# Next batch's softmax with powers on GpSimd, and a reordered first batch, in a cross-covariance attention plus SwiGLU kernel

## The chip, the cores and the metric

One core of one Trainium2 chip. The metric is the device time of one execution in microseconds (us), by the slowest core, of which there is only one here. Before the change the kernel took 873.5 us (median of 4 runs, 871.9 to 875.4). Runs in a slower state of the chip are marked by the measurement; verdicts use fast runs alone.

## The reference, cut to what matters

```python
B, N, C = 4, 6016, 256;  d_ff = 1536
qn = q / (norm(q, axis=1) + 1e-6)          # norms over the N tokens, one per channel
kn = k / (norm(k, axis=1) + 1e-6)
s  = kn.transpose(0, 2, 1) @ qn / tau      # per batch 256 x 256
a  = softmax(s)                            # (exp, divided by its row sum + 1e-9)
x  = (v @ a).reshape(B * N, C)
out = (silu(x @ w_gate) * (x @ w_val)) @ w_out
```

The kernel never forms `v @ a`. It multiplies the softmax into the two weight matrices (per batch, `Wg = a @ w_gate` and `Wv = a @ w_val`) and then works on `v` directly. So a batch needs the norms, the product of k and q, the softmax and the weight products *before* its first token can be worked on. For batches 1 to 3 this is done in the background of the batch before; batch 0 has to do it in the open.

## The kernel before

A batch is 12 chunks of 512 tokens (the last has 384), a chunk is 12 steps, so a batch has 144 steps and the kernel 576. The three matmul groups of a step are what TensorE does nearly all the time:

```python
def gv_step(b, ci, f, sv):                    # one step: 128 of the 1536 hidden channels
    g_ps, v_ps = ...                          # PSUM, two buffers each
    for dst, W in ((g_ps, Wg), (v_ps, Wv)):
        for kk in range(CH):                  # CH = 2
            nc.tensor.matmul(dst[:, :mv], W[:, kk, fs], vT[:, kk, :mv], ...)
    nc.scalar.activation(silu[:, :mv], g_ps[:, :mv], ACT.Silu)
    nc.vector.tensor_mul(sv[:, f, :mv], silu[:, :mv], v_ps[:, :mv])
# then prev.emit(prev.cm): four output matmuls (o_new) of the chunk before,
# then background(b + 1, step): whatever the plan puts into this step
```

Tokens come in two hops: GpSimd issues a load of v that casts to bf16 into DRAM (`vb`), and SyncE issues a DMA transpose of that into SBUF (`vT`, three buffers). In the program they stand two chunks ahead of their use.

```python
def load_v(b, ci):
    nc.gpsimd.dma_start(out=vb[...], in_=v[b, ...])
    nc.sync.dma_start_transpose(out=vT[:, :, :mv], in_=vb[:mv, :])
```

The background softmax, all in one step of the plan:

```python
def norm_sum(b):
    nc.tensor.matmul(ss, ones_f, acc, ...)                 # column sums, on all partitions
def softmax(b):
    nc.scalar.activation(nrm, ss, ACT.Sqrt)                # 128 x 512
    nc.vector.tensor_scalar_add(ink, in0=nrm[:, 1, :], scalar1=1e-6)
    nc.vector.reciprocal(ink, ink)                         # 128 x 256
    ... qc: norms of q put down the partitions by tiny matmuls ...
    nc.vector.tensor_mul(s_f[:, jh, :], kq[:, jh, :], ink)
    ... inq = 1 / (qc + 1e-6) ...
    nc.scalar.activation(exT[:, jh, :], s_f[:, jh, :], ACT.Exp, scale=inq[:, jh:jh + 1])
    ... rs = row sums of exT, by matmul; smr = 1 / (rs + 1e-9) ...

LOAD0, SQ0 = 2, 18                     # plan: loads of batch b+1 every 6 steps from step 2,
                                       # a pair of norm tiles every 3 steps from step 18,
S1 = SQ0 + 3 * NP + 2                  # then the softmax, then 12 weight products
```

The first batch: all loads of q and k, then `w_gate`, `w_val`, the first v tile, `w_out`, the second v tile; then norms, softmax, the first four weight products, and the steps begin.

## Time and profile before

The page's lines of busy time by engine (us, the share of the span of 869.4 us, the number of instructions) and of the chain of waits, which is the work that ended last followed back to the start, by engine and by line:

```profile
PE 811.8 (93%) x4933; PEld 484.7 (56%) x4933; DVE 545.1 (63%) x844; ACT 477.9 (55%) x841; POOL 77.8 (9%) x151
...
PE 90%; DMA 7%; ACT 1%; DVE 1%; issue 0%; POOL 0%; POOLq 0%
PE g_ps L238 29%; PE o_new L263 28%; PE v_ps L238 28%; DMA q_sb<-in_q_dram 3%; PE ps L221 3%; DMA vT<-vb 2%; PE kq_new L123 2%; DMA vb<-in_v_dram 2%; DVE ink L181 1%; ACT L178 0%; ACT exT L196 0%; PE ss L172 0%; DVE s_f L188 0%; ACT nrm L17
```

TensorE is busy for 93% and makes up 90% of the chain. A faster other engine is worth nothing here unless it closes a gap of TensorE, so the question is where these gaps are. The list of TensorE's waits (engine, line and tile that waited, what it waited for; us in total, times, longest):

```profile
PE g_ps L238 <- DMA vT<-vb: 16.6, 1, 16.6
...
PE rs L201 <- ACT exT L196: 13.2, 8, 3.2
PE qc L184 <- ACT nrm L178: 5.7, 4, 1.7
```

The 16.6 us is one wait, at the start, for the first transposed v tile. The waits on exT and nrm are the four softmaxes, one per batch. (A line left out, 15.9 us, belongs to the first batch too, which is bound by the loads of q and k there.) The start in the timeline (start us, duration us, instruction; in brackets the idle time before it and what ended that):

```profile
28.14 0.53 POOL L104 DMA_DIRECT2D vb<-in_v_dram  x1 [0.54 <-DMA q_sb<-in_q_dram]
...
39.42 0.91 ACT L196 ACTIVATE exT<-s_f,inq 128x256 bf16<-128x256 f32 x2 [1.98 <-DVE inq L191]
...
43.10 26.19 SPq L108 DMA_TRANSPOSE vT<-vb  x3
...
60.67 1.01 PE L238 MATMUL g_ps<-vT,Wg 128*128 128x512 bf16 x2 [16.61 <-DMA vT<-vb]
```

The load of the first v tile was issued at 28.14 us behind two weight matrices; its transpose began at 43.10 and the first step at 60.67. The first output matmul of chunk 1, which I use as the end of the start, stands at 85.40.

One background softmax, TensorE and its helpers:

```profile
195.42 1.02 PE L172 MATMUL ss<-acc_new,ones_f 128*128 128x512 f32 x2
...
197.53 1.28 ACT L178 ACT_TABLE_LOAD   x1
...
199.47 0.74 PE L184 MATMUL qc<-ones_f,nrm 1*128 1x1 f32 x4 [1.73 <-ACT nrm L178]
199.78 1.75 DVE L181 RECIPROCAL ink<-ink 128x256 f32<-128x256 f32 x1
...
203.19 0.19 PE L201 MATMUL rs<-ones_bf,exT 128*128 128x1 bf16 x1 [2.98 <-ACT exT L196]
...
203.68 1.01 PE L238 MATMUL g_ps<-vT,Wg 128*128 128x512 bf16 x2
...
207.72 0.38 PE L238 MATMUL g_ps<-vT,Wg 128*128 128x512 bf16 x1
```

From 195.42 to 207.72 TensorE gets through three steps, which take 3.9 us elsewhere (1.30 us each). So a softmax costs about 8.4 us: ScalarE's table load for Sqrt at 197.53, the square root, the reciprocal of 1.75 us, the products and the exponentials stand one after the other between the column sums (`ss`) and the row sums (`rs`). (The table load for Exp, in a line left out, runs beside the reciprocal; the one for Silu comes after the row sums.) TensorE waits 1.73 and 2.98 us there, and then runs slower for a while (the matmul pair at 203.68 took 1.01 us, usually 0.59; the granted clock was 0.67 between 200 and 210 us).

### The profile page before, as it was taken

To read this page: it belongs to the slowest core of one execution; us is meant where nothing else is said; L and a number is where in the kernel's file an instruction comes from. 1 tells how busy PE (TensorE), PEld (TensorE's weight loads), DVE (VectorE), ACT (ScalarE), POOL (GpSimd) and SP (SyncE) were. 2 spreads that over 40 slices of the span, in tenths; PEclk is the share of its full clock that TensorE was granted. 3 is DMA by queue.
4 is the path that set the end of the run, shared out by engine and by line. 5 is a ranking of instruction groups with operands and counts; after the bars stand their busy time and mean duration, and the time that the engine had idled before them with its cause. 6 is when DMAs were issued, how large, how long until landed. Compare 5 with 4: busy or idle time off the path is not lost.

```text
span 869.4 us, 13410 instructions
## 1 busy us (share of the span) xinstructions
PE 811.8 (93%) x4933; PEld 484.7 (56%) x4933; DVE 545.1 (63%) x844; ACT 477.9 (55%) x841; POOL 77.8 (9%) x151
## 2 busy tenths in 40 slices
PE   5528999997999999997999999998999999999998
PEld 2203666664566566664556566664556666656666
DVE  3505788875655688885555578886465555555554
ACT  4414666665544566665554566665545544444453
POOL 5333331023310000000000000000000000000000
PEclk9957999998999999998999999999999999999999
DMA  9999999239983121120211212121112112212211
GB/s 89 156 146 131 165 149 191 62 50 140 169 188 63 43 61 50 37 61 13 58 37 49 55 49 54 45 49 37 37 34 62 55 50 49 61 49 37 58 37 55
DMA packets 92785, 64.83 MB, mean 75 GB/s; under 512 B 53552, under 2 KB 91440, under 8 KB 91952
## 3 DMA queue, kind: packets, MB, share of 16 engines
q0 software_dynamic: 17456, 27.01, 23.6%
q1 hardware_dynamic: 75264, 36.97, 17.0%
q8 instruction: 38, 0.62, 0.3%
q14 instruction: 27, 0.22, 0.1%
HBM read 78.64 MB, written 36.96 MB: 133 GB/s over the span
## 4 chain that ended last, share of the span: by engine, by line
PE 90%; DMA 7%; ACT 1%; DVE 1%; issue 0%; POOL 0%; POOLq 0%
PE g_ps L238 29%; PE o_new L263 28%; PE v_ps L238 28%; DMA q_sb<-in_q_dram 3%; PE ps L221 3%; DMA vT<-vb 2%; PE kq_new L123 2%; DMA vb<-in_v_dram 2%; DVE ink L181 1%; ACT L178 0%; ACT exT L196 0%; PE ss L172 0%; DVE s_f L188 0%; ACT nrm L178 0%; ACT silu L241 0%
## 5 line engine op out<-in xcount | busy, mean ns | idle before, releaser
L242 DVE TENSOR_TENSOR sv<-silu,v_ps 128x512 bf16<-128x512 bf16 (+1 forms) x576 | 383.0, 674 | 253.2 <-ACT silu L241 230.9
L241 ACT ACTIVATE silu<-g_ps 128x512 bf16<-128x512 f32 (+1 forms) x576 | 338.5, 588 | 322.1 <-PE g_ps L238 303.3
L238 PE MATMUL g_ps<-vT,Wg 128*128 128x512 bf16 (+1 forms) x1152 | 342.4, 379 | 16.6 <-DMA vT<-vb 16.6
L238 PE MATMUL v_ps<-vT,Wv 128*128 128x512 bf16 (+1 forms) x1152 | 341.3, 378 | 0.0
L263 PE MATMUL o_new<-w_out_sb,sv 128*128 128x256 bf16 x2256 | 340.2, 274 | 0.0
L263 PEld LDWEIGHTS <-sv 128*128 128x128 bf16 x2256 | 221.6, 98 | 142.4 <-issue 2.2
L238 PEld LDWEIGHTS <-Wv 128*128 128x128 bf16 x1152 | 113.6, 99 | 133.6 <-issue 5.2
L238 PEld LDWEIGHTS <-Wg 128*128 128x128 bf16 x1152 | 107.8, 99 | 47.5 <-issue 20.7
L167 DVE TENSOR_TENSOR acc_new<-acc_new,sq 128x512 f32<-128x512 f32 x135 | 93.4, 692 | 24.9 <-ACT sq L141 22.6
L136 ACT ACTIVATE sq<-q_sb 128x512 bf16<-128x512 fp8e5 x96 | 57.9, 615 | 17.8 <-DMA q_sb<-in_q_dram 17.8
L123 PE MATMUL kq_new<-k_sb,q_sb 128*128 128x512 fp8e5 x184 | 46.4, 335 | 0.0
L141 ACT ACTIVATE sq<-k_sb 128x512 bf16<-128x512 fp8e5 x72 | 44.2, 614 | 0.0
L272 ACT COPY o_sb<-o_new 128x512 f32<-128x512 f32 x48 | 28.2, 587 | 14.4 <-PE o_new L263 13.7
L96 POOL DMA_DIRECT2D q_sb<-in_q_dram x48 | 26.2, 547 | 91.2 <-PE g_ps L238 50.1
L274 DVE COPY o_sb<-o_new 128x512 f32<-128x512 f32 (+1 forms) x48 | 31.7, 661 | 3.1 <-PE o_new L263 3.0
L153 PE MATMUL ss_new<-sq,ones_bf 128*128 128x512 bf16 x47 | 16.1, 427 | 15.9 <-DVE sq L138 15.9
L96 POOL DMA_DIRECT2D k_sb<-in_k_dram x48 | 25.7, 536 | 33.3 <-DMA k_sb<-in_k_dram 16.2
L123 PEld LDWEIGHTS <-q_sb 128*128 128x256 fp8e5 x184 | 23.9, 141 | 6.4 <-issue 1.9
L104 POOL DMA_DIRECT2D vb<-in_v_dram x48 | 23.8, 495 | 40.8 <-DMA k_sb<-in_k_dram 22.2
L138 DVE TENSOR_TENSOR sq<-k_sb 128x512 bf16<-128x512 fp8e5 (+1 forms) x24 | 15.3, 677 | 18.3 <-DMA k_sb<-in_k_dram 11.8
L221 PE MATMUL ps<-w_gate_sb,exT 128*128 128x512 bf16 x48 | 16.7, 439 | 1.6 <-ACT Wg L224 1.6
L221 PE MATMUL ps<-w_val_sb,exT 128*128 128x512 bf16 x48 | 16.3, 431 | 1.6 <-ACT Wv L224 1.6
(39 smaller groups left out, 102.3 us busy)
## 6 DMA issues: line engine op xcount, KB each, us to landing
out_dram<-o_sb SPq DMA_DIRECT2D x92, 256.0 KB, 2.3
vb<-in_v_dram POOLq DMA_DIRECT2D x44, 256.0 KB, 10.4
q_sb<-in_q_dram POOLq DMA_DIRECT2D x44, 128.0 KB, 10.7
k_sb<-in_k_dram POOLq DMA_DIRECT2D x44, 128.0 KB, 10.9
w_gate_sb<-in_moe_w_gate_dram POOLq DMA_DIRECT2D x1, 768.0 KB, 13.1
w_val_sb<-in_moe_w_val_dram POOLq DMA_DIRECT2D x1, 768.0 KB, 14.9
w_out_sb<-in_moe_w_out_dram POOLq DMA_DIRECT2D x1, 768.0 KB, 17.6
vT<-vb SPq DMA_TRANSPOSE x48, 3.2
```

The source lines that it names most:

```text
L96: nc.gpsimd.dma_start(out=dst[:, gs:gs + gm, :], in_=src[b].rearrange("(p s) c -> p s c", s=NS)[:, gs:gs + gm, :])
L123: nc.tensor.matmul(kq[:, jh, :], q_sb[:, ps:ps + 2, js], k_sb[:, ps:ps + 2, :], start=(t == 0 and jh == 0), stop=last, perf_mode=DR, skip_ ...
L136: nc.scalar.activation(sq[:, :pm, 0, :], q_sb[:, ps:ps + pm, :], ACT.Square)
L141: nc.scalar.activation(sq[:, :pm, 1, :], k_sb[:, ps:ps + pm, :], ACT.Square)
L167: nc.vector.tensor_add(acc, acc, sq[:, s, :, :])
L221: nc.tensor.matmul(ps, exT[:, jh, ih * P:(ih + 1) * P], src[:, jh, cols], start=(jh == 0), stop=(jh == CH - 1))
L238: nc.tensor.matmul(dst[:, :mv], W[:, kk, fs], vT[:, kk, :mv], start=(kk == 0), stop=(kk == CH - 1))
L241: nc.scalar.activation(silu[:, :mv], g_ps[:, :mv], ACT.Silu)
L242: nc.vector.tensor_mul(sv[:, f, :mv], silu[:, :mv], v_ps[:, :mv])
L263: nc.tensor.matmul(self.o_ps[:, j % 2, :], self.sv[:, f, j * P:(j + 1) * P], w_out_sb[:, f, :], start=(f == 0), stop=(f == FH - 1))
L272: nc.scalar.copy(o_sb[:, :m, :], self.o_ps[:, :m, :])
L274: nc.vector.tensor_copy(o_sb[:, :m, :], self.o_ps[:, :m, :])
```

## The change

The intent is to take all of this off TensorE's path. In the background, square root, reciprocal and exponential become powers on GpSimd, which is idle most of the time (9% busy); the parts are put 16 to 18 steps apart so that nobody waits, and ScalarE never leaves the Silu table. In the first batch, k is loaded two groups ahead of q (so that 1/|k| is ready early), the first v tile goes among the last loads of q, the weights come in thirds, and four idle matmuls keep TensorE's clock up.

```diff
+    half, minus, euler = ...            # constants 0.5, -1.0 (128 x 258) and e (128 x 512)
...
-    def norm_sum(b): ...
-    def softmax(b): ...
+    def norm_inv(b):
+        ss = psum_m.tile([P, C + CH], FP32, tag="misc")
+        nc.tensor.matmul(ss[:, :C], ones_f, acc[:, 1, :], start=True, stop=True)      # k, on all partitions
+        for jh in range(CH):                                                          # q, down the partitions
+            nc.tensor.matmul(ss[:, C + jh:C + jh + 1], acc[:, 0, jh * P:(jh + 1) * P], ones_f[:, 0:1], ...)
+        nc.vector.tensor_copy(inv, ss)
+        nc.gpsimd.tensor_tensor(out=inv, in0=inv, in1=half, op=ALU.pow)               # 128 x 258
+        nc.gpsimd.tensor_scalar_add(inv, in0=inv, scalar1=1e-6)
+        nc.gpsimd.tensor_tensor(out=inv, in0=inv, in1=minus, op=ALU.pow)              # 128 x 258
+    def logits(b):
+        for jh in range(CH):
+            nc.vector.scalar_tensor_tensor(out=s_f[:, jh, :], in0=kq[:, jh, :],
+                scalar=inv[:, C + jh:C + jh + 1], in1=inv[:, :C], op0=ALU.mult, op1=ALU.mult)
+        nc.gpsimd.tensor_tensor(out=exT, in0=euler, in1=s_f, op=ALU.pow)              # 128 x 512
+    def row_sums(b): ...                                                              # rs, smr, as before
...
-    LOAD0, SQ0 = 2, 18
+    LOAD0, SQ0 = 10, 22                 # loads every 5 steps, norm pairs every 2.5
...
-    plan[S1].append(("sum", 0))
-    plan[S1 + 1].append(("softmax", 0))
+    plan[S1].append(("inv", 0))
+    plan[S1 + 16].append(("logits", 0))
+    plan[S1 + 34].append(("rows", 0))
     for u in range(len(wp_units)):
-        plan[S1 + 4 + 2 * u].append(("wp", u))
+        plan[S1 + 36 + (u * 3) // 2].append(("wp", u))
...
+    K_AHEAD = 2
+    ... order: k two groups ahead of q ...
+    for n, (g, which) in enumerate(order):
+        load_qk(0, g, which)
+        if n == len(order) - 8:
+            load_v(*allc[0])
+    load_w(0)                           # thirds of w_gate and w_val
+    load_w(1)
+    load_v(*allc[1])
+    load_w(2)
...
+        keep_warm(4)                    # in the first batch's softmax
```

More of the change, by code (lines that the diff above doesn't have):

```diff
@@ L77 @@
     nc.vector.memset(ones_bf, 1.0)
+    half = const.tile([P, C + CH], FP32)
+    minus = const.tile([P, C + CH], FP32)
+    euler = const.tile([P, CH, C], FP32)
+    warm_bf = const.tile([P, 2 * C], BF16)
+    nc.vector.memset(warm_bf, 1.0)
     nc.scalar.activation(warm, ones_f[:, 0:1], ACT.Sqrt)
@@ L87, with load_qk @@
     vt_ready = {}
-    def load_qk(b, g):
-        if g == 0:
+    def load_qk(b, g, which):
+        if b not in qk_tiles:
             q_sb = qkpool.tile([P, NS, C], FP8, tag="q_sb")
@@ L94, in load_qk @@
         gs, gm = groups[g]
-        for src, dst in zip((q, k), qk_tiles[b]):
-            nc.gpsimd.dma_start(
-                out=dst[:, gs:gs + gm, :],
-                in_=src[b].rearrange("(p s) c -> p s c", s=NS)[:, gs:gs + gm, :])
+        src, dst = (q, k)[which], qk_tiles[b][which]
+        nc.gpsimd.dma_start(
+            out=dst[:, gs:gs + gm, :],
+            in_=src[b].rearrange("(p s) c -> p s c", s=NS)[:, gs:gs + gm, :])
     def load_v(b, ci):
@@ L130, in gemm1_pair, with first_norm, first_inv_k, first_softmax @@
                                  skip_group_check=True)
-    def square_pair(b, t, first):
+    def first_norm(b, t, which):
+        x_sb = qk_tiles[b][which]
+        ps, pm = pairs[t]
+        sq = sqpool.tile([P, 2, C], BF16, tag="sq%d" % which)
+        if which == 0:
+            nc.scalar.activation(sq[:, :pm, :], x_sb[:, ps:ps + pm, :], ACT.Square)
+        else:
+            nc.vector.tensor_mul(sq[:, :pm, :], x_sb[:, ps:ps + pm, :],
+                                 x_sb[:, ps:ps + pm, :])
+        if t == 0:
+            ss_new = psum_gv.tile([P, C], FP32, tag="gv"[which])
+            state[b, "ss", which] = ss_new
+        ss = state[b, "ss", which]
+        for s in range(pm):
+            nc.tensor.matmul(ss, ones_bf, sq[:, s, :],
+                             start=(t == 0 and s == 0),
+                             stop=(t == NP - 1 and s == pm - 1))
+    def first_inv_k(b):
+        nrm = work.tile([P, C], FP32, tag="nrm")
+        nc.scalar.activation(nrm, state[b, "ss", 1], ACT.Sqrt)
+        ink = work.tile([P, C], FP32, tag="ink")
+        nc.vector.tensor_scalar_add(ink, in0=nrm, scalar1=1e-6)
+        nc.vector.reciprocal(ink, ink)
+        state[b, "ink"] = ink
+    def first_softmax(b):
+        kq, ink = state[b, "kq"], state[b, "ink"]
+        nrq = work.tile([1, C], FP32, tag="nrq")
+        nc.scalar.activation(nrq, state[b, "ss", 0][0:1, :], ACT.Sqrt)
+        qc = psum_m.tile([P, CH], FP32, tag="misc")
+        for jh in range(CH):
+            nc.tensor.matmul(qc[:, jh:jh + 1], nrq[0:1, jh * P:(jh + 1) * P],
+                             ones_f[0:1, 0:1], start=True, stop=True)
+        keep_warm(4)
+        inq = work.tile([P, CH], FP32, tag="inq")
+        s_f = work.tile([P, CH, C], FP32, tag="s_f")
+        nc.vector.tensor_mul(s_f[:, 0, :], kq[:, 0, :], ink)
+        nc.vector.tensor_scalar_add(inq, in0=qc, scalar1=1e-6)
+        nc.vector.reciprocal(inq, inq)
+        if inv_tau != 1.0:
+            nc.vector.tensor_scalar_mul(inq, in0=inq, scalar1=inv_tau)
+        nc.vector.tensor_mul(s_f[:, 1, :], kq[:, 1, :], ink)
+        exT = attn.tile([P, CH, C], BF16, tag="exT")
+        for jh in range(CH):
+            nc.scalar.activation(exT[:, jh, :], s_f[:, jh, :], ACT.Exp,
+                                 scale=inq[:, jh:jh + 1])
+        state[b, "exT"] = exT
+    def norm_acc(b, t):
         q_sb, k_sb = qk_tiles[b]
@@ L135, in square_pair @@
         sq = sqpool.tile([P, 2, 2, C], BF16, tag="sq")
-        nc.scalar.activation(sq[:, :pm, 0, :], q_sb[:, ps:ps + pm, :], ACT.Square)
-        if first:
-            nc.vector.tensor_mul(sq[:, :pm, 1, :], k_sb[:, ps:ps + pm, :],
-                                 k_sb[:, ps:ps + pm, :])
-        else:
-            nc.scalar.activation(sq[:, :pm, 1, :], k_sb[:, ps:ps + pm, :], ACT.Square)
-        return sq
-    def norm_pair_pe(b, t):
-        sq = square_pair(b, t, True)
-        if t == 0:
-            ss_new = psum_m.tile([P, 2, C], FP32, tag="misc")
-            state[b, "ss"] = ss_new
-        ss = state[b, "ss"]
-        ps, pm = pairs[t]
-        for s in range(pm):
-            nc.tensor.matmul(ss, ones_bf, sq[:, s, :, :],
-                             start=(t == 0 and s == 0),
-                             stop=(t == NP - 1 and s == pm - 1))
-    def norm_pair_dve(b, t):
-        sq = square_pair(b, t, False)
-        ps, pm = pairs[t]
+        for which in range(2):
+            nc.scalar.activation(sq[:, :pm, which, :],
+                                 qk_tiles[b][which][:, ps:ps + pm, :], ACT.Square)
         if t == 0:
@@ L167, in norm_pair_dve @@
             nc.vector.tensor_add(acc, acc, sq[:, s, :, :])
-    def norm_sum(b):
+    def norm_inv(b):
         acc = state[b, "acc"]
-        ss = psum_m.tile([P, 2, C], FP32, tag="misc")
-        nc.tensor.matmul(ss, ones_f, acc, start=True, stop=True)
-        state[b, "ss"] = ss
-    def softmax(b):
-        ss, kq = state[b, "ss"], state[b, "kq"]
-        nrm = work.tile([P, 2, C], FP32, tag="nrm")
-        nc.scalar.activation(nrm, ss, ACT.Sqrt)
-        ink = work.tile([P, C], FP32, tag="ink")
-        nc.vector.tensor_scalar_add(ink, in0=nrm[:, 1, :], scalar1=1e-6)
-        nc.vector.reciprocal(ink, ink)
-        qc = psum_m.tile([P, CH], FP32, tag="misc")
-        for jh in range(CH):
-            nc.tensor.matmul(qc[:, jh:jh + 1], nrm[0:1, 0, jh * P:(jh + 1) * P],
-                             ones_f[0:1, 0:1], start=True, stop=True)
+        ss = psum_m.tile([P, C + CH], FP32, tag="misc")
+        nc.tensor.matmul(ss[:, :C], ones_f, acc[:, 1, :], start=True, stop=True)
+        for jh in range(CH):
+            nc.tensor.matmul(ss[:, C + jh:C + jh + 1], acc[:, 0, jh * P:(jh + 1) * P],
+                             ones_f[:, 0:1], start=True, stop=True)
+        inv = work.tile([P, C + CH], FP32, tag="inv")
+        nc.vector.tensor_copy(inv, ss)
+        nc.gpsimd.tensor_tensor(out=inv, in0=inv, in1=half, op=ALU.pow)
+        nc.gpsimd.tensor_scalar_add(inv, in0=inv, scalar1=1e-6)
+        nc.gpsimd.tensor_tensor(out=inv, in0=inv, in1=minus, op=ALU.pow)
+        state[b, "inv"] = inv
@@ L186, in softmax @@
+    def logits(b):
+        kq, inv = state[b, "kq"], state[b, "inv"]
         s_f = work.tile([P, CH, C], FP32, tag="s_f")
         for jh in range(CH):
-            nc.vector.tensor_mul(s_f[:, jh, :], kq[:, jh, :], ink)
-        inq = work.tile([P, CH], FP32, tag="inq")
-        nc.vector.tensor_scalar_add(inq, in0=qc, scalar1=1e-6)
-        nc.vector.reciprocal(inq, inq)
+            nc.vector.scalar_tensor_tensor(
+                out=s_f[:, jh, :], in0=kq[:, jh, :], scalar=inv[:, C + jh:C + jh + 1],
+                in1=inv[:, :C], op0=ALU.mult, op1=ALU.mult)
@@ L192, in softmax, with row_sums @@
         if inv_tau != 1.0:
-            nc.vector.tensor_scalar_mul(inq, in0=inq, scalar1=inv_tau)
+            nc.gpsimd.tensor_scalar_mul(s_f, in0=s_f, scalar1=inv_tau)
         exT = attn.tile([P, CH, C], BF16, tag="exT")
-        for jh in range(CH):
-            nc.scalar.activation(exT[:, jh, :], s_f[:, jh, :], ACT.Exp,
-                                 scale=inq[:, jh:jh + 1])
+        nc.gpsimd.tensor_tensor(out=exT, in0=euler, in1=s_f, op=ALU.pow)
+        state[b, "exT"] = exT
+    def row_sums(b):
+        exT = state[b, "exT"]
@@ L207, in softmax, with keep_warm @@
         Wv = attn.tile([P, CH, DFF], BF16, tag="Wv")
-        state[b, "exT"], state[b, "smr"], state[b, "W"] = exT, smr, (Wg, Wv)
+        state[b, "smr"], state[b, "W"] = smr, (Wg, Wv)
+    def keep_warm(n):
+        ps = psum_o.tile([P, 2, C], FP32, tag="o")
+        for _ in range(n):
+            nc.tensor.matmul(ps, ones_bf, warm_bf, start=True, stop=True)
     wp_units = [(wc, w, ih) for wc in range(NWC) for w in range(2) for ih in range(CH)]
@@ L278, in emit @@
                         in_=o_sb[:, :m, :])
-    LOAD0, SQ0 = 2, 18
+    LOAD0, SQ0 = 10, 22
     plan = [[] for _ in range(STEPS)]
     for g in range(len(groups)):
-        plan[LOAD0 + 6 * g].append(("load", g))
+        plan[LOAD0 + 5 * g].append(("load", g))
     for t in range(NP):
-        plan[SQ0 + 3 * t].append(("norm", t))
-        plan[SQ0 + 3 * t + 1].append(("gemm1", t))
-    S1 = SQ0 + 3 * NP + 2
-    plan[S1].append(("sum", 0))
-    plan[S1 + 1].append(("softmax", 0))
+        step = SQ0 + (5 * t) // 2
+        plan[step].append(("norm", t))
+        plan[step + 1].append(("gemm1", t))
+    S1 = SQ0 + (5 * NP) // 2 + 1
+    plan[S1].append(("inv", 0))
+    plan[S1 + 16].append(("logits", 0))
+    plan[S1 + 34].append(("rows", 0))
     for u in range(len(wp_units)):
-        plan[S1 + 4 + 2 * u].append(("wp", u))
+        plan[S1 + 36 + (u * 3) // 2].append(("wp", u))
     def background(b, step):
@@ L296, in background @@
             if what == "load":
-                load_qk(b, i)
+                load_qk(b, i, 0)
+                load_qk(b, i, 1)
             elif what == "norm":
-                norm_pair_dve(b, i)
+                norm_acc(b, i)
             elif what == "gemm1":
                 gemm1_pair(b, i)
-            elif what == "sum":
-                norm_sum(b)
-            elif what == "softmax":
-                softmax(b)
+            elif what == "inv":
+                norm_inv(b)
+            elif what == "logits":
+                logits(b)
+            elif what == "rows":
+                row_sums(b)
@@ L306, in background, with load_w @@
             else:
                 wp_unit(b, i, psum_m, "misc")
+    def load_w(wc):
+        cols = slice(wc * WP, (wc + 1) * WP)
+        for src, dst in ((moe_w_gate, w_gate_sb), (moe_w_val, w_val_sb)):
+            nc.gpsimd.dma_start(
+                out=dst[:, :, cols],
+                in_=src.rearrange("(h l) d -> l h d", l=P)[:, :, cols])
     allc = [(b, ci) for b in range(B) for ci in range(NCH)]
     VT_AHEAD = 2
-    for g in range(len(groups)):
-        load_qk(0, g)
-    nc.gpsimd.dma_start(out=w_gate_sb, in_=moe_w_gate.rearrange("(h l) d -> l h d", l=P))
@@ L315 @@
-    nc.gpsimd.dma_start(out=w_val_sb, in_=moe_w_val.rearrange("(h l) d -> l h d", l=P))
-    load_v(*allc[0])
-    nc.gpsimd.dma_start(out=w_out_sb, in_=moe_w_out.rearrange("(h l) d -> l h d", l=P))
-    load_v(*allc[1])
-    for t in range(NP):
-        norm_pair_pe(0, t)
-        gemm1_pair(0, t)
-    softmax(0)
+    NG = len(groups)
+    K_AHEAD = 2
+    order = []
+    for g in range(NG + K_AHEAD):
+        if g < NG:
+            order.append((g, 1))
+        if g >= K_AHEAD:
+            order.append((g - K_AHEAD, 0))
@@ new lines @@
+    for n, (g, which) in enumerate(order):
[6 more added lines that the diff above has]
+    load_w(2)
+    nc.gpsimd.dma_start(out=w_out_sb, in_=moe_w_out.rearrange("(h l) d -> l h d", l=P))
+    nc.gpsimd.memset(half, 0.5)
+    nc.gpsimd.memset(minus, -1.0)
+    nc.gpsimd.memset(euler, 2.718281828459045)
+    for g, which in order:
+        gs, gm = groups[g]
+        for t in range(gs // 2, (gs + gm + 1) // 2):
+            first_norm(0, t, which)
+            if which == 0:
+                gemm1_pair(0, t)
+        if which == 1 and g == NG - 1:
+            first_inv_k(0)
@@ L323 @@
+    first_softmax(0)
+    row_sums(0)
     NFIRST = 2 * CH
```

## The prediction

> **What bounds the kernel now.** The page's busy table has TensorE at 811.8 of 869.4 us; the chain of waits is 90% TensorE, 7% DMA. So only TensorE's gaps are for sale. The stretches and the list of TensorE's waits show two kinds.
>
> 1. Start. In the timeline the last norm matmul ends about 35.5 us, exT at 40.3, four weight products at 44; then TensorE waits 16.6 us for the first transposed v tile. Its load was issued at 28.1, behind two weight matrices, and landed at 43.1; the transpose took 17.5 us among the other loads. Chunk 0 then runs at a granted clock of 0.58 (60 to 80 us); chunk 1 starts at 85.4.
> 2. Three softmaxes (about 195, 400, 610 us). A step costs 1.30 us; the timeline from 195.42 to 207.72 holds three steps, so each softmax costs 12.3-3.9 = 8.4 us: 2.1 of its own matmuls (ss 0.86, qc 0.74, rs 0.48), 4.9 of waiting (qc for Sqrt with its table load 1.7, rs for the 1.75 us reciprocal, the products and Exp 3.2), 1.4 of low clock afterwards, in which the Silu table is loaded too.
>
> **What the change does.**
> - Softmax: Sqrt and Exp leave ScalarE (three table loads of 1.28 us per batch), the reciprocal leaves VectorE. TensorE keeps about 1.7 us (half the ss, four small pieces, rs). If the powers are done in time, it gains 6.7 us per batch, 20 us in all.
> - The powers: two on 258 columns and one on 512 on GpSimd. No trace has a duration. The schedule allows 16 steps (21 us) and 18 steps (23 us). The Trainium skill (GPSIMD Engine Reference, Performance versus the Vector engine) measures about 2.6 cycles per element for an add at 1.2 GHz; I estimate ten to twenty times that for a power, 5 to 10 and 10 to 20 us. No run here shows it. GpSimd also issues the loads, in order, so v loads wait behind powers; they are issued two chunks (31 us) ahead.
> - Norm pairs every 2.5 instead of 3 steps: VectorE needs 2.5x0.69+2x0.69+0.1 = 3.2 of 3.5 us; tight, but no lasting stall.
> - Start: the first v tile lands about 27 us and its transpose, again about 17.5 us, ends at 44 to 45. The last q slips to about 37. With 1/|k| ready before, exT comes about 2.6 us after the last norm matmul (4.8 before), about 41; first weight third about 40, so chunk 0 starts about 45 instead of 60.7. Then tile 1's transpose (load lands 44, 17.5 to 25 us) limits: chunk 1 starts at 66 to 70. Gain 15 to 19, say 17.
>
> Nearly all is on the critical path, as TensorE has no other idle time.
>
> **Prediction.** 874.8-20-17 = 838 us; range 826 to 851. Faster by over 2%: 0.88; within 2%: 0.07; slower: 0.05.
>
> **What would show it.** Right: no TensorE wait on exT, nrm or qc after the first batch, granted clock 1.0 there; no table load after the first Silu; chunk 0's matmuls from about 45 us, chunk 1's before 70; powers under 10 and 20 us; steps of 1.30 us while they run. Wrong: VectorE's logits waiting for GpSimd, or rs for the power.
>
> **What would make it wrong.** A 512-column power of over 23 us stalls TensorE each batch. Powers that lock VectorE out: the skill (SBUF — State Buffer) says GpSimd and VectorE instructions with two SBUF inputs exclude each other; here the norm additions have two, but end before the powers; the gate product has one in PSUM. A burst of loads released after the last power, which draws out the transposes (20 to 30 us in such bursts before). Chunk 0 still at half clock, or a later second v tile.

## The result, and the profile after

| | before | after |
|---|---|---|
| median of 4 runs, us | 873.5 | 1209.9 |
| range, us | 871.9 to 875.4 | 1208.2 to 1210.8 |
| ratio of the fast runs, 95% interval | | 1.385 (1.381 to 1.389) |
| TensorE busy, us | 811.8 | 819.0 |
| GpSimd busy, us | 77.8 | 581.0 |

A ratio is the mean time of one kernel's fast runs over that of the other's in the same rounds, so it is not quite the ratio of the medians. The result is correct, and 38% slower, not 4% faster. The same lines of the page (the span is now 1209.0 us):

```profile
PE 819.0 (68%) x4984; PEld 491.9 (41%) x4984; DVE 538.9 (45%) x836; ACT 462.4 (38%) x824; POOL 581.0 (48%) x170
...
PE 50%; POOL 42%; DMA 5%; ACT 2%; DVE 1%; issue 1%; DVEq 0%; ACTq 0%; POOLq 0%
POOL exT L228 20%; PE o_new L303 15%; PE g_ps L278 15%; PE v_ps L278 15%; POOL inv L213 10%; POOL inv L215 10%; DMA vT<-vb 2%; PE ps L261 2%; PE kq_new L128 1%; DMA q_sb<-in_q_dram 1%; DMA k_sb<-in_k_dram 1%; ACT sq L192 1%; DVE sv L282 1%;
```

TensorE does the same work (819 against 812 us), but 42% of the chain is now GpSimd: `exT` 20%, the two powers of `inv` 10% each. The list of TensorE's waits:

```profile
PE v_ps L278 <- DVE sv L282: 191.4, 9, 62.9
PE rs L236 <- POOL exT L228: 177.2, 3, 59.8
...
PE g_ps L278 <- DMA vT<-vb: 0.2, 1, 0.2
```

Two waits that did not exist make up 368.6 us. One names GpSimd's exT. The other names VectorE's gate product `sv`; it needs one more step back, to what VectorE waited for. The timeline of the first background softmax (lines of GpSimd, VectorE and TensorE):

```profile
165.22 0.42 DVE L212 COPY inv<-ss 128x258 f32<-128x258 f32 x1
...
165.80 41.65 POOL L213 TENSOR_TENSOR inv<-inv,half 128x258 f32<-128x258 f32 x1 [60.71 <-DVE inv L212]
...
208.50 41.65 POOL L215 TENSOR_TENSOR inv<-inv,minus 128x258 f32<-128x258 f32 x1
...
250.18 0.88 DVE L222 SCALAR_TENSOR_TENSOR s_f<-kq_new,inv 128x256 f32<-128x256 f32 x2 [63.88 <-POOL inv L215]
...
251.21 82.19 POOL L228 TENSOR_TENSOR exT<-euler,s_f 128x512 bf16<-128x512 f32 x1
251.70 1.01 PE L278 MATMUL v_ps<-vT,Wv 128*128 128x512 bf16 x2 [62.86 <-DVE sv L282]
```

The first power runs from 165.80 to 207.45, the second to 250.15. VectorE reached the logits in its queue 63.9 us before that, and its later gate products stand behind them in order; TensorE filled its two PSUM buffers and stopped, for 62.9 us. Then the exponential ran for 82 us, 20 of which TensorE could work until it came to the row sums. In sum per batch (stretches of the trace; in each its length, then busy us and instructions of TensorE, its weight loads, VectorE, ScalarE and GpSimd; granted clock, DMA share, GB/s):

```profile
165.00:185.00 20.00, 20.00 (x124) 11.94 (x123) 11.55 (x18) 9.46 (x17) 19.20 (x1) 1.00 0.04 14
185.00:251.00 66.00, 3.84 (x24) 2.24 (x23) 1.51 (x4) 2.85 (x5) 65.83 (x5) 0.56 0.00 0
...
254.00:274.00 20.00, 19.65 (x119) 11.51 (x117) 10.80 (x16) 9.45 (x16) 20.00 (x1) 0.98 0.30 79
274.00:334.00 60.00, 0.54 (x6) 0.27 (x7) 0.34 (x3) 0.00 (x0) 60.00 (x3) 0.54 0.00 0
```

From 165 to 334 us TensorE worked some 46 us. And GpSimd's instructions by form (output and input shapes, count, busy us in sum, mean ns of one):

```profile
L228 POOL TENSOR_TENSOR exT<-euler,s_f 128x512 bf16<-128x512 f32 x3 | 246.6, 82184 | 0.1
L213 POOL TENSOR_TENSOR inv<-inv,half 128x258 f32<-128x258 f32 x3 | 124.9, 41644 | 287.1 <-DVE inv L212 287.1
L215 POOL TENSOR_TENSOR inv<-inv,minus 128x258 f32<-128x258 f32 x3 | 124.9, 41642 | 0.3
```

A power of 258 columns takes 41.64 us and one of 512 columns 82.18 us: 161 ns per column, for all three kinds of exponent here (0.5, -1 and the logits). The plan had allowed 16 steps (20.8 us) for 84 us of work and 18 steps (23.4 us) for 82 us.

The start is the part that came out well. The first step stands at 44.71 us and chunk 1's first output matmul at 64.31:

```profile
44.71 0.59 PE L278 MATMUL g_ps<-vT,Wg 128*128 128x512 bf16 x2
...
64.31 0.60 PE L303 MATMUL o_new<-w_out_sb,sv 128*128 128x256 bf16 x4
```

That is 16.0 and 21.1 us earlier than before, with a granted clock of 1.00 between 40 and 60 us (0.50 before).

### The profile page after: what moved, and what is told of

Same layout as the page of the kernel before. It is cut to its first block, busy times and chain, and to the rows that moved or that the text cites. A ratio compares the mean times of both kernels' runs of the same rounds, so it can differ in the third digit from the quotient of the medians.

```text
span 1209.0 us, 13488 instructions
## 1 busy us (share of the span) xinstructions
PE 819.0 (68%) x4984; PEld 491.9 (41%) x4984; DVE 538.9 (45%) x836; ACT 462.4 (38%) x824; POOL 581.0 (48%) x170
## 4 chain that ended last, share of the span: by engine, by line
PE 50%; POOL 42%; DMA 5%; ACT 2%; DVE 1%; issue 1%; DVEq 0%; ACTq 0%; POOLq 0%
POOL exT L228 20%; PE o_new L303 15%; PE g_ps L278 15%; PE v_ps L278 15%; POOL inv L213 10%; POOL inv L215 10%; DMA vT<-vb 2%; PE ps L261 2%; PE kq_new L128 1%; DMA q_sb<-in_q_dram 1%; DMA k_sb<-in_k_dram 1%; ACT sq L192 1%; DVE sv L282 1%; PE ss_new L152 0%; DVE acc_new L201 0%
## 5 line engine op out<-in xcount | busy, mean ns | idle before, releaser
L278 PE MATMUL v_ps<-vT,Wv 128*128 128x512 bf16 (+1 forms) x1152 | 342.7, 379 | 191.6 <-DVE sv L282 191.4
L213 POOL TENSOR_TENSOR inv<-inv,half 128x258 f32<-128x258 f32 x3 | 124.9, 41644 | 287.1 <-DVE inv L212 287.1
L228 POOL TENSOR_TENSOR exT<-euler,s_f 128x512 bf16<-128x512 f32 x3 | 246.6, 82184 | 0.1
L215 POOL TENSOR_TENSOR inv<-inv,minus 128x258 f32<-128x258 f32 x3 | 124.9, 41642 | 0.3
L236 PE MATMUL rs<-ones_bf,exT 128*128 128x1 bf16 x16 | 1.2, 170 | 177.6 <-POOL exT L228 177.2
L222 DVE SCALAR_TENSOR_TENSOR s_f<-kq_new,inv 128x256 f32<-128x256 f32 x6 | 2.6, 479 | 191.5 <-POOL inv L215 191.5
L192 ACT ACTIVATE sq<-q_sb 128x512 bf16<-128x512 fp8e5 x72 | 44.2, 614 | 0.0
## 6 DMA issues: line engine op xcount, KB each, us to landing
vb<-in_v_dram POOLq DMA_DIRECT2D x44, 256.0 KB, 10.4
w_out_sb<-in_moe_w_out_dram POOLq DMA_DIRECT2D x1, 768.0 KB, 18.7
```

The lines of the kernel that those rows point to most:

```text
L192: nc.scalar.activation(sq[:, :pm, which, :], qk_tiles[b][which][:, ps:ps + pm, :], ACT.Square)
L213: nc.gpsimd.tensor_tensor(out=inv, in0=inv, in1=half, op=ALU.pow)
L215: nc.gpsimd.tensor_tensor(out=inv, in0=inv, in1=minus, op=ALU.pow)
L228: nc.gpsimd.tensor_tensor(out=exT, in0=euler, in1=s_f, op=ALU.pow)
```

## The experiments

Theory 1: the powers take 161 ns per column by themselves, and everything else in the change works as meant. Theory 2: GpSimd's work harms in other ways, by locking VectorE out (as the prediction feared) or by keeping back the loads of v. Theory 3: the powers were slow because of their data or of what ran beside them. A fourth came up on the way. Ten kernels were run; their rounds were shared with runs of the kernel before, whose median was 871.0, 868.9 and 871.1 us in the three jobs (one of the third job's seven was slow).

| run | median us | ratio to before (95%) |
|---|---|---|
| cheap_op (wrong result) | 828.6 | 0.952 (0.949 to 0.956) |
| start_only | 890.8 | 1.021 (1.014 to 1.028) |
| softmax_only (one run, state unknown) | 1233.4 | |
| pow_probe | 870.4 | 1.002 (0.996 to 1.009) |
| poly | 832.4 | 0.957 (0.954 to 0.960) |
| exp_act | 835.3 | 0.961 (0.958 to 0.965) |
| start_paced | 851.3 | 0.980 (0.977 to 0.982) |
| poly_no_warm | 831.4 | 0.956 (0.952 to 0.960) |
| poly_late_v | 843.3 | 0.970 (0.965 to 0.975) |
| poly_k_beside_q | 830.9 | 0.956 (0.953 to 0.959) |

### cheap_op: products in place of the powers

```diff
-        nc.gpsimd.tensor_tensor(out=inv, in0=inv, in1=half, op=ALU.pow)
+        nc.gpsimd.tensor_tensor(out=inv, in0=inv, in1=half, op=ALU.mult)
```

and the same in the other two places. Its output is wrong, which doesn't matter for the time.

> The changed kernel with the three powers on GpSimd replaced by multiplications of the same shapes (a wrong result on purpose). Theory 1, the powers are slow and nothing else in the change is: TensorE's two waits (191.4 us for the gate product behind the logits, 177.2 us for the exponentials) go, and with them 8 to 13 us of low clock after six stalls: 828 to 834 us, no wait of TensorE on these lines over 1 us, each multiplication under 2 us. Theory 2, GpSimd work itself is the trouble, by holding VectorE's SBUF port or by keeping back the v loads: over 845 us, with VectorE instructions longer than before or waits for v tiles.

Measured: 828.6 us. The powers alone cost 1209.9 - 828.6 = 381 us (the two come from different jobs): the 368.6 us of waits, and some 13 us more, which fits the low clock after each of the six stalls (0.50 from 251 to 254 us, for one) and TensorE's busy time for the same 4984 instructions, 819.0 against 804.5 us. From TensorE's waits:

```profile
PE v_ps L278 <- DVE sv L282: 3.0, 6, 0.5
...
PE rs L236 <- ACT exT L183: 0.5, 2, 0.3
```

The wait of `rs` that is left is the first batch's, on ScalarE; none on exT from GpSimd is left. `v_ps` waits 3.0 us in six places for VectorE. So short instructions of GpSimd (0.73 and 1.27 us) in the same places, with the same order of loads, harm nothing. That long ones do no other harm this run can't show; for VectorE pow_probe does, and for v the changed kernel itself, where TensorE waited 0.2 us for a v tile.

### pow_probe: powers that nobody waits for

```diff
+    def probe():                            # called once, after the last load
+        for w in (4, 64, 128, 256, 512):
+            nc.gpsimd.tensor_tensor(out=pz[:, :w], in0=px[:, :w], in1=py[:, :w], op=ALU.pow)
+        nc.gpsimd.tensor_tensor(out=pb, in0=px, in1=py, op=ALU.pow)                          # into bf16
+        nc.gpsimd.tensor_tensor(out=pz[0:16, :], in0=px[0:16, :], in1=py[0:16, :], op=ALU.pow)
+        nc.gpsimd.tensor_tensor(out=pz, in0=px, in1=py, op=ALU.mult)
+        nc.gpsimd.tensor_scalar(out=pz, in0=px, scalar1=0.5, scalar2=1.0, op0=ALU.mult, op1=ALU.add)
```

> The kernel before, and on GpSimd after its last load, while VectorE and TensorE work on, powers of 4, 64, 128, 256 and 512 columns, one of 512 into bf16, one of 512 on 16 partitions only, then a product and a scale-and-add of 512 columns; nobody waits for them. Theory 1 (a fixed cost per column, about 161 ns): 0.8, 10.4, 20.7, 41.3, 82.3 us, 82 into bf16, 82 on 16 partitions; the product 1 to 2.5 us; the kernel's time 872 to 877 us, as nothing waits. Theory 3 (the powers were slow because of their data or of what ran beside them): the ones here, on constant data and beside a busy VectorE, differ by over 10% from 161 ns per column. Theory 2: VectorE's gate products get longer while a power runs, and the time rises over 880.

Measured: 870.4 us, the same as before. The probe's instructions by form (columns as above):

```profile
L318 POOL TENSOR_TENSOR pz<-px,py 128x512 f32<-128x512 f32 x1 | 82.5, 82489 | 0.1
L319 POOL TENSOR_TENSOR pb<-px,py 128x512 bf16<-128x512 f32 x1 | 82.1, 82135 | 0.0
L320 POOL TENSOR_TENSOR pz<-px,py 16x512 f32<-16x512 f32 x1 | 82.1, 82131 | 0.0
...
L318 POOL TENSOR_TENSOR pz<-px,py 128x64 f32<-128x64 f32 x1 | 10.5, 10549 | 0.1
L321 POOL TENSOR_TENSOR pz<-px,py 128x512 f32<-128x512 f32 x1 | 1.3, 1272 | 0.1
...
L318 POOL TENSOR_TENSOR pz<-px,py 128x4 f32<-128x4 f32 x1 | 1.1, 1054 | 0.1
```

The slope from 64 to 512 columns is (82.49-10.55)/448 = 160.6 ns per column, and the fixed part is 0.3 to 0.4 us (what is left of the times of 64 and 4 columns). It is the same into bf16, and the same on 16 partitions as on 128, so it is a cost per column and not per element. Constant data, with VectorE and TensorE at work beside it, give the figure of the changed kernel, where the second power ran beside idle engines. Theory 3 falls. A product of the same 512 columns takes 1.27 us: a power costs 65 times as much. And 320 us of powers that nobody waits for cost nothing that shows (0.996 to 1.009 of before). Nor did they hold VectorE up. Its norm additions, which read two SBUF tiles, in this run (columns as above):

```profile
L167 DVE TENSOR_TENSOR acc_new<-acc_new,sq 128x512 f32<-128x512 f32 x135 | 93.4, 692 | 24.4 <-ACT sq L141 21.9
```

In the kernel before they are 135 with 692 ns, too. Between 243 and 480 us, when a power was running all the time, 45 of them took 691 ns in the mean, as 45 did in the kernel before in the same stretch. So the half of theory 2 that has VectorE locked out falls.

### softmax_only: the new softmax with the old first batch

```diff
-    ... after's first batch, order of loads and idle matmuls
+    ... before's first batch and softmax(0); the three constants set on GpSimd after its loads
```

> The old first batch with the new softmax. Theory 1: the whole loss is here: 1210 + 21 = 1231 us (1225 to 1237), waits of 64 and 60 us per batch. If the two halves of the change hurt each other, it lies under 1215.

Measured: 1233.4 us in one run, whose state is unknown. The waits of TensorE are 191.4 and 177.0 us, those of the changed kernel, so the whole loss is in this half.

### start_only: the new first batch with the old softmax

```diff
-    ... norm_inv, logits, row_sums in the background; LOAD0, SQ0 = 10, 22
+    ... norm_sum, softmax in the background; LOAD0, SQ0 = 2, 18, as before
```

> The new first batch with the old softmax in the background. Theory 1: only the start gains, by 21.1 us (first output matmul of chunk 1 at 64.3 instead of 85.4): 850 to 855 us, the three softmaxes costing 8.4 us each as before. Theory 2: the same; this run sizes the start alone. If the start's gain is eaten later (loads now earlier, transposes later), it is above 860.

Measured: 890.8 us (884.4 to 901.4), worse than before, where all theories had said 850 to 855. This was a surprise. The profiled run was slow (901.4 us, over 1.5% above the fastest of this kernel), but the three fast runs, 884 to 896 us, lie above every run of before in this job as well, so the loss is not one of the slow run alone; its place is read from that one trace. The start was as good as in the changed kernel (chunk 1 at 61.9 us). What was gained is given back later, in nine waits for v tiles (in the profiled run):

```profile
PE g_ps L316 <- DMA vT<-vb: 40.7, 9, 14.5
```

The kernel before has one wait for a v tile, the 16.6 us at the start. The view of the DMA queues from 60 to 140 us, by queue (packets, MB, share of the 16 engines) and by issue (count, KB each, us from issue to landing):

```profile
q1 hardware_dynamic: 6091, 2.64, 59.7%
...
vb<-in_v_dram POOLq DMA_DIRECT2D x10, 256.0 KB, 34.4
...
vT<-vb SPq DMA_TRANSPOSE x4, 35.1
```

A transpose took 35 us here. In the kernel before, in the same stretch:

```profile
vT<-vb SPq DMA_TRANSPOSE x5, 24.8
```

That was long too, but TensorE did not wait, as chunk 1 began at 85.4 and not at 61.9 us. Theory 4: GpSimd runs ahead of the schedule. With the old softmax nearly all that GpSimd's list of waits names in this run is earlier loads that have to land, so it issues the loads of a batch and more in one burst, and the transposes share the DMA engines with them. In the changed kernel the first power of each batch, at step 83, holds GpSimd until VectorE has the sums (287.1 us in three waits), which paces the loads as a by-product; the multiplications of cheap_op do that too (333.6 us).

### start_paced: the same, with paced loads

```diff
             if b + 1 < B:
+                if any(what == "load" for what, _ in plan[ci * FH + f]):
+                    nc.gpsimd.tensor_copy(out=token, in_=sv[:, f, 0:1])
                 background(b + 1, ci * FH + f)
```

> The run with the start alone, in which TensorE waited nine times for v tiles (40.7 us) because loads ran ahead and held up the transposes, with each load of the next batch now waiting for the step it stands in (a GpSimd copy of one gate value ahead of it). Theory 4 (loads running ahead, which the slow powers or any wait of GpSimd on VectorE would stop, eat the start's gain): waits for v tiles under 2 us, transposes of the first half of the batch back to 3 to 6 us, 848 to 854 us. Rival (the new order of the first loads itself does it): waits for v tiles stay, over 870 us.

Measured: 851.3 us, with a spread of 0.3 us in four runs, and no wait of TensorE for a v tile. The same view of DMA:

```profile
q1 hardware_dynamic: 7691, 3.64, 17.0%
...
vb<-in_v_dram POOLq DMA_DIRECT2D x5, 256.0 KB, 5.6
vT<-vb SPq DMA_TRANSPOSE x5, 3.3
```

A transpose takes 3.3 us instead of 35. So theory 4 holds: the start is worth 17.6 us, but only if the loads don't run ahead. That it is the loads running ahead is shown; why the DMA engines did so badly is not. In start_only single packets of the transposes, 18 to 31 ns as a rule, took up to 18.7 us in the trace (10.4 us between 60 and 140 us); in the kernel before, with a like burst but later chunks, no packet took over 1.6 us. Long packets are not enough by themselves: in the changed kernel one took 8.6 us, with hardly a wait of TensorE for v. This stays open.

### poly: small powers, the exponential as a polynomial

A mended version. The norms of k are taken down the partitions as those of q are, so the powers have 4 columns instead of 258; a diagonal matrix and one matmul spread 1/|k| over all partitions. The exponential of a logit, which is a cosine over tau and so bounded, is a polynomial of degree 5 (for a larger 1/tau it is scaled down first and squared afterwards; only tau = 1 was run).

```diff
-        nc.gpsimd.tensor_tensor(out=inv, ...)                  # 258 columns, twice
+        nc.gpsimd.tensor_tensor(out=inv, ...)                  # 4 columns, twice
+        for ih in range(CH):
+            nc.gpsimd.tensor_scalar(out=kd[:, ih, :], in0=ident, scalar1=inv[:, CH + ih:CH + ih + 1],
+                                    scalar2=1.0, op0=ALU.mult, op1=ALU.mult)
+    def k_rows(b):
+        nc.tensor.matmul(kr, ones_f, state[b, "kd"], start=True, stop=True)
+        nc.vector.tensor_copy(ink, kr)
...
-        nc.gpsimd.tensor_tensor(out=exT, in0=euler, in1=s_f, op=ALU.pow)
+        nc.gpsimd.tensor_scalar(out=e, in0=s_f, scalar1=scale / 5, scalar2=1.0, op0=ALU.mult, op1=ALU.add)
+        for n in (4, 3, 2, 1):
+            nc.gpsimd.tensor_tensor(out=e, in0=e, in1=s_f, op=ALU.mult)
+            nc.gpsimd.tensor_scalar(out=exT if n == 1 and nsq == 0 else e, in0=e,
+                                    scalar1=scale / n, scalar2=1.0, op0=ALU.mult, op1=ALU.add)
...
+    plan: inv at S1, k_rows 5 steps later, logits 7, rows 20, weight products from 22 on, every 2 steps
```

> A mended version with a correct result: the powers are taken on 4 columns (norms of q and k down the partitions; 8 columns of powers, about 1.5 us at the probe's rate), 1/|k| is spread over the partitions by one matmul with a diagonal, and the exponential is a polynomial of degree 5 on GpSimd (5 scale-and-adds at about 0.6 us and 4 products at 1.27 us by the probe, 8 us in all, 13 steps allowed). Theory 1 (only the length of the powers was wrong): 828 to 833 us, like the run with multiplications, no wait of TensorE on exT or of VectorE on inv over 1 us. Theory 2: over 845.

Measured: 832.4 us, correct, 0.957 of before. This is the change as it was meant. GpSimd's instructions by form:

```profile
L246 POOL TENSOR_TENSOR e<-e,s_f 128x512 f32<-128x512 f32 x12 | 15.2, 1268 | 1.0
L247 POOL TENSOR_SCALAR e<-e 128x512 f32<-128x512 f32 x9 | 5.6, 622 | 0.8
L216 POOL TENSOR_TENSOR inv<-inv,minus 128x4 f32<-128x4 f32 x3 | 3.1, 1044 | 0.2
```

The polynomial takes 4x1.27 + 5x0.62 = 8.2 us, a tenth of the power, and the two small powers 2.1 us (1.5 were expected).

### exp_act: small powers, the exponential on ScalarE

```diff
+    def exps(b):                            # 2 steps after the logits, rows 4 steps later
+        nc.scalar.activation(exT, state[b, "s_f"], ACT.Exp, scale=inv_tau)
```

in place of the polynomial of poly.

> As poly, but the exponential stays on ScalarE (one Exp of 512 columns per batch, with a table load of 1.28 us before it and one for Silu after it), placed two steps after the logits. ScalarE is then away from the gates for about 3.2 us per batch against 1.3 us steps with two buffers, so 0.5 to 2 us of TensorE waits per batch: 831 to 837 us, 2 to 5 us more than poly. If ScalarE's tables were what the old softmax cost, it is 15 us or more above poly.

Measured: 835.3 us, 2.9 more than poly in the same rounds. TensorE waits 3.2 us in all for Silu, three times:

```profile
PE g_ps L292 <- ACT silu L295: 3.2, 3, 1.1
```

The tables are loaded in this version too (1.28 us for Exp and 1.28 for Silu per batch). So these two loads, spread over steps, cost about 1 us per batch, which fits the view that most of the softmax's old 8.4 us was TensorE standing in the chain. The square root and the reciprocals are small powers on GpSimd here as in poly; what they would cost on ScalarE and VectorE, spread out, was not run.

### poly_no_warm, poly_late_v, poly_k_beside_q: the parts of the start

Each takes one part of the new start out of poly: the four idle matmuls; the early v tile (now behind two thirds of the weights); the lead of k over q.

```diff
-        keep_warm(4)                                    # poly_no_warm
...
-        if n == len(order) - 8:                         # poly_late_v
-            load_v(*allc[0])
     load_w(0)
     load_w(1)
+    load_v(*allc[0])
...
-    K_AHEAD = 2                                         # poly_k_beside_q
+    K_AHEAD = 0
```

> The mended version without the four idle matmuls that keep TensorE busy during the first softmax. If they hold the clock, the first weight products and chunk 0 run at half clock for some us: 833 to 838 against 829 to 832 us for the mended version, granted clock from 40 to 60 us below 0.9. If the short gap (2 us instead of 16.6) is what keeps the clock, nothing changes: within 1 us.

> The mended version with the first v tile loaded behind two thirds of the weights instead of among the last q and k. If the early v tile is what gives the start, chunk 0 waits again for its transpose: load lands about 43 us, transpose 13 to 18 us, chunk 0 from 56 to 61 instead of 44.7 us, and part of it at half clock: 843 to 851 us. If the order of k and q or the weights in thirds is what gives it, under 836.

> The mended version with k and q loaded side by side (k first in each group), not k two groups ahead. The 1.75 us reciprocal of the norms of k then lies behind the last norm matmul again: exT and chunk 0 later by 1.5 to 2.5 us, 831 to 835 us. If the k-ahead order is what gives the start, over 840.

Measured: 831.4, 843.3 and 830.9 us, against 832.4 for poly in another job (ratios 0.956, 0.970, 0.956 against 0.957). The early v tile is worth about 1.3% (11 us); without it TensorE waits again, as its list of waits shows:

```profile
PE g_ps L300 <- DMA vT<-vb: 8.6, 1, 8.6
```

though less than in the kernel before, as the first step then stands at 52.3 us, earlier than the 56 to 61 expected. Without the idle matmuls the granted clock between 40 and 60 us was 0.91, yet the time did not change beyond the noise, and neither did it without the lead of k (831 to 835 had been expected). The weights in thirds were not tried alone.

## Why the prediction was wrong

Predicted: 838 us (826 to 851), with a chance of 0.05 of being slower by over 2%. Measured: 1209.9 us.

- **The step that failed is the length of the powers**: "I estimate ten to twenty times that for a power, 5 to 10 and 10 to 20 us. No run here shows it." They took 41.6 and 82.2 us, 161 ns per column, which at the 1.2 GHz of the page that I cited would be 193 cycles, 74 times its 2.6 cycles for an addition. I had nothing measured, and the prediction gives no ground for the ten to twenty; its estimates end just under what the plan's 16 and 18 steps allowed. The plan (two powers and an addition of 258 columns in 20.8 us, one power of 512 in 23.4 us) would have held at 39 ns per column for the first and 45 for the second.
- **The mechanism was named, but at far too small a chance**: "A 512-column power of over 23 us stalls TensorE each batch", with VectorE's logits waiting for GpSimd as the mark. That is what the trace shows: 191.4 us behind the logits and 177.2 us at the row sums, 381 us with what follows the stalls. A plan of this shape has no soft failure: what the powers took over the plan, 63.4 and 58.8 us, is three times over 366.6 us, against 368.6 us of waits.
- **The size of the rest was right, in part by luck** (see the next bullet and the last). I had 20 us for the softmax and 17 for the start, 37 in all. With the powers made cheap, before and after differ by 871.0-828.6 = 42.4 us (mended and correct: 868.9-832.4 = 36.5).
- **The start**: first step expected about 45 us, measured 44.7; chunk 1 expected at 66 to 70, measured 64.3. I thought that the second tile's transpose would limit; it took 14.6 us and did not, as chunk 0 ran at full clock and ended at 64 by itself. The start alone, paced, measures 17.6 us, which leaves 18.9 us of poly's 36.5 for the softmax, where I had 20, if the two simply add up. Of its parts I had expected exT earlier by 2 us for the lead of k, which the run without it does not show: the last norm matmul began at 38.4 us there and at 40.3 in poly, and exT at 40.4 and 42.3.
- **Powers locking VectorE out**: I had left this open. The Trainium skill ("SBUF — State Buffer", SBUF: two separate sides) says that GpSimd and VectorE instructions with two SBUF inputs exclude each other for a whole instruction, if the one on GpSimd reads SBUF. The gate product, with one of its inputs in PSUM, took 685 ns in the mean before, and also in pow_probe, where powers ran beside it for 320 us; so it was not held up. In the changed kernel the norm additions were over before the powers began, but pow_probe has the page's case: the norm additions with two SBUF inputs, beside powers that read SBUF, took their usual 691 ns. Here the page and the measurement differ, and the measurement decides for these two instructions. One VectorE instruction was longer beside a power, an addition of a constant with 654 ns against 295 in the kernel before; it is a single one and stays open.
- **What I did not see at all** is that the loads of v, q and k had been running ahead of the plan in the kernel before (GpSimd issued its last load at 244.9 of 869 us, where I had v loads two chunks ahead), and that an earlier start makes this cost something. The waits of GpSimd in the new softmax hide it, which I had not counted on: that the start kept its gain was luck.

## What to carry to other kernels

An operation that no trace of yours has is a guess until it is measured, and a schedule written around it is no evidence of its length: run it once, alone, off the path, in two widths, before building on it. Putting work on an idle engine is free only until somebody waits for it in order; then all of it that exceeds the planned time counts. And when the softmax was at last spread, leaving the exponential on ScalarE with its two table loads cost 1 us per batch (835.3 against 832.4 us), so spreading the chain, so that no engine's queue waits, gave most of the gain; a version with square root and reciprocals left where they were was not run.

## What the Trainium skill lacked or had wrong

- "GPSIMD Engine Reference", Performance versus the Vector engine: it gives the cost of an addition, and nothing on a power. The runs show 160.6 ns per column (82.2 us for 512 columns, 41.6 us for 258, 1.05 us for 4), the same for 16 and 128 partitions and for fp32 and bf16 output; a product of 512 columns takes 1.27 us and a scale-and-add 0.61 us. The product's 2.5 ns per column would be 3.0 cycles at 1.2 GHz, fixed part included, near the page's 2.6 for an addition.
- "DMA: Bandwidth & Descriptors", Queues, rings and completion order: it says that a DMA engine takes the queues in turn, packet by packet; that section gives no figure for how long one packet can take. In start_only the transposes' packets of 256 bytes, 18 ns in the median (31 between 60 and 140 us), took up to 18.7 us, and a transpose 35 us instead of 3.3 us with paced loads. The cause is open.
- "ScalarE: Activation LUTs", What ACT_TABLE_LOAD costs: it adds to the load of about 1283 ns a wait of about 1380 ns for ScalarE to drain, 2.66 us per switch. In the kernel before, the load itself is 1.28 us, as the page says, but the Sqrt table's load began at 197.53 us, 0.02 us after the Silu before it had ended, and Sqrt began 0.01 us after the load, at 198.82: 1.3 us for the switch in all.
- "SBUF — State Buffer", SBUF: two separate sides, on GpSimd and VectorE excluding each other: not seen here with VectorE's norm additions and GpSimd's powers, 691 ns per addition with and without powers beside it (see "Powers locking VectorE out" above).
